# Constants that travel behind the first group's values, and two weight blocks requested by ScalarE

## The chip, the core and the metric

The kernel runs on one NeuronCore of a Trainium2 chip. Its engines work in parallel, each through its own program in order: TensorE (PE, matrix products), VectorE (DVE), ScalarE (ACT), GpSimd (POOL) and SyncE (SP), which here only asks for transfers. The 16 DMA engines move the data. SBUF is the memory on the chip, PSUM the place where TensorE leaves sums. The metric is the device time of one execution in microseconds (us).

## The reference

```python
# retention: q, k, v are (B=4, H=8, S=768, D=64)
gamma = 1.0 - 2.0 ** (-5.0 - np.arange(H))
for t in range(S):
    state = gamma * state + k[t] (outer) v[t]      # per batch and head, D x D
    y[t] = q[t] @ state / sqrt(D)
x = y as (B, S, H * D)                             # 4 x 768 x 512
# gated MLP
h = relu(x @ w_in)                                 # w_in 512 x 1024
u, v = h[..., :512], h[..., 512:]
v_n = (v - mean(v)) / sqrt(var(v) + 1e-6)          # over the last axis
v_s = w_spatial @ v_n + b_spatial                  # w_spatial 768 x 768, over the sequence
out = (u * v_s) @ w_out                            # w_out 512 x 512
```

The weights come to the chip as 64-bit words (doubles) in 12 blocks of 128 x 512 and are split there into a high and a low single-precision part.

## The kernel before

The sequence of each batch is cut into 6 chunks of 128 positions, which makes 24 groups (batch, chunk). For a group two transfers of 512 KB come in: `qk` (keys and queries, transposed) and `vk` (values and keys, natural). The decay of retention is put into scale factors: the values are multiplied by one table before use (`scale_values`), the results by two others at eviction (`out_evict`). These small tables arrive in one transfer, `decay_t` (128 x 80 floats, 40 KB; 320 bytes in each partition). 72 of the 80 columns are the factors for values and for evictions, the last 8 are a compact form of a third table, which is spread on the chip: VectorE multiplies it with an identity pattern (`decay_rows`, output `sown`), TensorE sums it over partitions (`decay_spread`, output `spread`), ScalarE copies the result to `qd_t` (`decay_copy`).

The order of the work is written out by hand in a table, STEPS, of short words. A letter names a step, its digits the group, block or part; every engine runs its own instructions in the order of the words. The words that matter here are: `G` asks for a group's `qk` and `vk`; `v` is the transfer of the constants; `p` scales values (p0 and p1 on GpSimd); `U` gives filling matmuls `wps` on a tile of zeros; `q` and `j` are scores and mask; `L` asks for a block of weights (its tile is `raw`); `a` and `c` are the steps that split it (`room`, `df`), ScalarE first, then VectorE; `m` handles the third table; `t` adds a group to the running sums (`total`), `k` copies these to SBUF (`ws`), `y` makes the outputs (`x`), `E` evicts them (`xf`), `h` and `l` make their high and low parts (`xh`, `xl`), `V` starts the MLP's products.

The words around the change run, before: `G0 v p0 U10 q0 j0 L0 L2 a0 m2 t00 m0 k000 k001 t01 y00`. So ScalarE does a0 (first split step of block 0), then k000 and k001 (copies of the first sums); TensorE does the filling matmuls, q0, t00, m0 (`spread`), t01; and t01, which adds to the same PSUM tile, comes behind the copies of t00. All loads are asked for by SyncE, in the order of the words. Tiles of one tag rotate through a few buffers (`bufs`), so that a load into a buffer waits for the last reader of what was there: `qk` has three, `vk` two. Every third early group takes its `vk` in `third` instead. Large tiles with tags `sp0` to `sp13` hold other things later in the program.

Of the kernel before, what the change touches and what calls it, by code (L numbers as in the profile page):

```python
# [9 lines left out]
F32 = mybir.dt.float32  # L10
# [6 lines left out]
ALU = mybir.AluOpType  # L17
# [4 lines left out]


STEPS = (
# [71 lines left out]
def tile_retention_gmlp(  # L96
# [11 lines left out]
    nc = tc.nc  # L108
    P = 128
    B = out.shape[0]  # L110
    NG = groups.shape[0]
    NC = NG // B
    C = P // 2
    D = C
    NP = groups.shape[3] // (4 * (P // 2))
# [10 lines left out]
    rpool = ctx.enter_context(tc.tile_pool(name="ret", bufs=2))  # L126
# [6 lines left out]
    ND = 3 * NC * NP  # L133
    consts_t = wpool.tile([P, ND + NP * P // C], F32, name="decay_t")
    decay_t = consts_t[:, :ND].rearrange("p (n t h) -> p n t h", t=3, h=NP)
    vd_t, qg_t = decay_t[:, :, :2], decay_t[:, :, 2]
# [2 lines left out]

    mhalf = wpool.tile([P, 1], F32, name="mhalf")  # L140
    nc.gpsimd.memset(mhalf, 0.5)
    nc.scalar.mul(mhalf, mhalf, -1.0)

    winv_w = wpool.tile([P, KT, 2, DM], F32R, name="winv_w")
    winv_h, winv_l = winv_w[:, :, 0], winv_w[:, :, 1]
# [5 lines left out]
    keep = tc.keep_in_program_order  # L151
# [4 lines left out]
    def load(dst, src):  # L156
        keep(nc.sync.dma_start(dst, src))
# [4 lines left out]
    def pick(n):  # L162
        return (nc.gpsimd, nc.vector, nc.scalar)[int(n)]

    doubles = [
        (w[:, k, 0], w[:, k, 1], src[k])
        for w, src in ((winv_w, w_inv), (winu_w, w_inu), (wout_w, w_out))
        for k in range(KT)
    ]
    raws = {}  # L170

    def load_double(i):

        if i >= len(doubles):
            return
        if i < 3:
            if i == 0:
                raws["first"] = mpool.tile([P, 3, DM], I64, tag="vn", name="raw0", bufs=1)
            raws[i] = raws["first"][:, i]
        else:  # L180
            t = slot(STAGED[i], I64, f"raw{i}")
            raws[i] = t.rearrange("p s c -> p (s c)")[:, :DM]
        load(raws[i], doubles[i][2])

    HC = NC // 2

    def slot(n, dtype, name):

        cols = HALF // 2 if dtype == I64 else HALF
        return mpool.tile([P, HC, cols], dtype, tag=f"sp{n}", name=name, bufs=1)  # L190
# [88 lines left out]
    naturals = {}  # L279
    values = {}  # L280
    scores = {}
    states = {}
# [6 lines left out]
    def load_group(g):  # L289
        if g >= NG:  # L290
            return

        t = rpool.tile([P, 2, 2, NP, C], F32, tag="qk", name=f"qk{g}", bufs=3)
        load(t.rearrange("p s i h c -> p (s i h c)"), groups[g, 0])
        keys[g], queries[g] = t[:, 0], t[:, 1]
        if g < EARLY:
            load_values(g)

    EARLY = 9

    def load_values(g):
        if g >= NG:
            return
        if g < EARLY and g % 3 == 2:
            t, w = (
                slot(n, F32, f"third{g}_{n}").rearrange("p s c -> p (s c)")[:, : 4 * NP * C]
                for n in THIRD
            )
            t, w = (x.rearrange("p (s i h c) -> p s i h c", s=2, i=2, h=NP) for x in (t, w))
        else:  # L310
            t = rpool.tile([P, 2, 2, NP, C], F32, tag="vk", name=f"vk{g}", bufs=2)
            w = rpool.tile([P, 2, 2, NP, C], F32, tag="ws", name=f"ws{g}", bufs=2)
        load(t.rearrange("p s i h c -> p (s i h c)"), groups[g, 1])
        values[g], naturals[g] = t[:, 0], t[:, 1]
        scores[g], states[g] = w[:, 0], w[:, 1]

    def scale_values(g, engine=None):
        engine = engine or nc.gpsimd
        if engine is nc.scalar:
            for i in range(2):  # L320
                for hp in range(NP):
                    v, f = values[g][:, i, hp], vd_t[:, g % NC, i, hp : hp + 1]
                    keep(nc.scalar.mul(v, v, f))  # L323
            return
        vd = vd_t[:, g % NC].unsqueeze(3).broadcast_to([P, 2, NP, D])
        keep(engine.tensor_tensor(values[g], values[g], vd, ALU.mult))  # L326

    total = {}
# [384 lines left out]
    def warm(n):  # L713
# [3 lines left out]
    splits = split_clamp, split_shift, split_sign, split_power, split_low  # L717

    steps = {
        "m": lambda n: (decay_spread, decay_copy, decay_rows)[n](),  # L720
        "v": lambda n: load(consts_t, decay),
        "B": lambda n: load(bsp_t, b_sp),
        "L": load_double,
        "K": load_spatial,
        "G": load_group,
        "J": load_values,
        "a": split_top,
        "c": lambda n: splits[n % 10](n // 10),
        "H": split_high,
        "R": lambda n: split_rest(n % 100, pick(n // 100)),  # L730
        "Q": lambda n: split_sum(n % 100, pick(n // 100)),
        "p": lambda n: scale_values(n % 100, pick(n // 100)),
        "q": ret_scores,
        "j": ret_mask,
# [59 lines left out]
            eye_t[r], eye_t[r], [[1, C]], ALU.is_equal, 0.0, base=0, channel_multiplier=-1  # L794
        )

    def decay_rows():
        n = NP * P // C
        eye = eye_t.unsqueeze(2).broadcast_to([P, C, n])
        own = consts_t[:, ND:].unsqueeze(1).broadcast_to([P, C, n])  # L800
        rows = rows_t.rearrange("p (c n) -> p c n", n=n)
        keep(nc.vector.tensor_tensor(rows, eye, own, ALU.mult))

    def decay_spread():
        spread[0] = ps_m.tile([P, NP * P], F32, tag="m", name="spread")
# [6 lines left out]
    for n in ROOMS:  # L812
        t = slot(n, F32, f"room{n}").rearrange("p s c -> p (s c)")
        rooms += [t[:, :DM], t[:, DM : 2 * DM]]

    for word in STEPS.split():
        steps[word[0]](int(word[1:] or 0))

# [85 lines left out]
```

## Time and profile before

| What | Value |
|---|---|
| median of 3 runs | 371.31 us (370.73 to 371.78) |
| the profiled execution | 370.93 us |
| its span, first to last instruction | 369.1 us |
| busy: TensorE, VectorE, ScalarE, GpSimd | 362.0, 240.1, 155.8, 114.2 us |
| granted TensorE clock, mean | 0.999 |
| moved by DMA | 41.20 MB, 112 GB/s over the span |

The busy times say that TensorE has almost no room. They are sums over the whole program; whether the start has other limits than the rest is seen only in views of single stretches.

### The profile page before, as it was taken

The page shows a single profiled execution, that of the slowest core. Times are in us where ns is not written, and L with a number is a line of the kernel's source. Part 1 is how long each engine was busy: PE and PEld are TensorE (multiplying, and loading weights), DVE is VectorE, ACT ScalarE, POOL GpSimd, SP SyncE. Part 2 cuts the span into 40 slices and gives each one's busy share as a digit, 9 for nine tenths or more (in the row PEclk, how much of TensorE's full clock was granted, in tenths as well). Part 3 has the DMA queues.
Part 4 walks back from the last instruction along what each step waited for, and adds up shares of the span by engine and source line. Part 5 has one row for each costly group of instructions (what it writes and reads, how often), then busy time and mean ns, then how long its engine had stood idle before and what let it go on. Part 6 is the DMA issues. An engine that isn't in the chain of part 4 may idle for free.

```text
span 369.1 us, 10329 instructions
## 1 busy us (share of the span) xinstructions
PE 362.0 (98%) x4428; PEld 315.1 (85%) x4428; DVE 240.1 (65%) x533; ACT 155.8 (42%) x321; POOL 114.2 (31%) x121
## 2 busy tenths in 40 slices
PE   7999999999999999999999999999999999999995
PEld 3678885879888889999988889999998888999884
DVE  2998999599866767797685563278585443165631
ACT  2798784443512455532223246242133244433232
POOL 3612621461053325243225341233142321404010
PEclk9999999999999999999999999999999999999999
DMA  7975886012343430303333114113304002000022
GB/s 279 409 263 202 290 333 247 0 33 83 103 158 115 173 123 24 116 2 115 115 117 143 58 59 144 44 73 115 118 0 141 6 0 87 0 0 2 1 87 85
DMA packets 13149, 41.20 MB, mean 112 GB/s; under 512 B 1584, under 2 KB 1840, under 8 KB 13104
## 3 DMA queue, kind: packets, MB, share of 16 engines
q1 hardware_dynamic: 12960, 40.42, 30.4%
q8 instruction: 35, 0.57, 0.7%
q10 hardware_dynamic: 144, 0.13, 0.1%
q14 instruction: 10, 0.08, 0.1%
HBM read 34.25 MB, written 6.29 MB: 110 GB/s over the span
## 4 chain that ended last, share of the span: by engine, by line
PE 96%; ACT 1%; DVE 1%; issue 0%; DVEq 0%
PE u L154 18%; PE v L154 18%; PE o L154 18%; PE y L154 10%; PE sp L154 8%; PE x L154 6%; PE z L154 5%; PE s L154 4%; PE w L154 3%; PE d L154 3%; PE wps L715 2%; PE total L154 1%; ACT third L323 1%; PE o_last L154 0%; ACT third L352 0%
## 5 line engine op out<-in xcount | busy, mean ns | idle before, releaser
L154 PE MATMUL u<-xh,winu_w 128*128 128x384 f32 x256 | 68.3, 338 | 0.0
L154 PE MATMUL v<-winv_w,xh 128*128 128x512 f32 x192 | 60.8, 398 | 0.0
L154 PE MATMUL o<-wout_w,gh 128*128 128x512 f32 (+1 forms) x192 | 59.7, 392 | 0.0
L449 DVE SCALAR_TENSOR_TENSOR xf<-x,decay_t,qd_t 128x128 f32<-128x128 f32 x96 | 29.2, 344 | 28.7 <-PE x L154 23.9
L154 PEld LDWEIGHTS u<-xh,winu_w 128*128 128x128 f32 x256 | 46.5, 188 | 0.7
L154 PE MATMUL u<-xl,winu_w 128*128 128x384 f32 x128 | 42.9, 335 | 0.0
L154 PE MATMUL y<-sp,a 128*128 128x384 f32 x216 | 42.1, 338 | 0.0
L154 PEld LDWEIGHTS v<-winv_w,xh 128*128 128x128 f32 x192 | 35.2, 188 | 7.5
L154 PEld LDWEIGHTS o<-wout_w,gh 128*128 128x128 f32 x192 | 35.2, 188 | 6.9
L547 POOL TENSOR_TENSOR vn<-vn 128x384 f32<-128x384 f32 x24 | 24.9, 1036 | 50.5 <-DVE a L160 41.6
L563 ACT CAST a<-vn 128x384 fp32r<-128x384 f32 x42 | 21.0, 512 | 42.8 <-POOL vn L547 27.3
L154 PEld LDWEIGHTS y<-sp,a 128*128 128x128 f32 x216 | 37.9, 188 | 0.5
L154 PE MATMUL v<-winv_w,xl 128*128 128x512 f32 x96 | 37.6, 392 | 0.0
L154 PE MATMUL o<-wout_w,gl 128*128 128x512 f32 (+1 forms) x96 | 37.3, 389 | 0.0
L326 POOL TENSOR_TENSOR vk<-vk,decay_t 128x512 f32<-128x512 f32 x18 | 19.7, 1094 | 39.4 <-DMA vk<-in_float_dram 35.8
L160 DVE TENSOR_TENSOR a<-vn,a 128x384 fp32r<-128x384 f32 x42 | 23.8, 580 | 12.5 <-ACT a L563 12.3
L513 POOL TENSOR_TENSOR rs<-rs,mhalf 128x1 f32<-128x1 f32 x24 | 15.0, 629 | 50.2 <-DVE rs L509 47.8
L624 ACT ACTIVATE ur<-u 128x384 f32<-128x384 f32 x32 | 15.2, 488 | 36.0 <-PE u L154 32.4
L500 DVE BATCH_NORM_STATS2 bst<-vr 128x6 f32<-128x512 f32 x24 | 16.4, 686 | 18.4 <-ACT vr L493 18.4
L154 PE MATMUL s<-qk 64*64 64x64 f32 x768 | 28.2, 221 | 0.0
L154 PEld LDWEIGHTS s<-qk 64*64 64x64 f32 x768 | 25.4, 136 | 2.7 <-issue 2.3
L402 DVE TENSOR_TENSOR ws<-d,ws 64x256 f32<-64x256 f32 x54 | 22.8, 422 | 6.5 <-PE d L154 5.0
(114 smaller groups left out, 671.7 us busy)
## 6 DMA issues: line engine op xcount, KB each, us to landing
qk<-in_float_dram SPq DMA_DIRECT2D x24, 512.0 KB, 4.8
vk<-in_float_dram SPq DMA_DIRECT2D x21, 512.0 KB, 4.6
raw<-in_int_dram SPq DMA_DIRECT2D x12, 512.0 KB, 6.9
out_dram<-ot SPq DMA_DIRECT2D x23, 256.0 KB, 2.1
wst<-in_float_dram SPq DMA_DIRECT2D x4, 576.0 KB, 8.6
third<-in_float_dram SPq DMA_DIRECT2D x3, 512.0 KB, 10.0
bsp_t<-in_float_dram SPq DMA_DIRECT2D x1, 384.0 KB, 6.8
out_dram<-ot SPq DMA_DIRECT2D x1, 128.0 KB, 2.0
```

Source lines behind the costliest of these rows:

```text
L154: keep(nc.tensor.matmul(out, lhs, rhs, start=start, stop=stop, skip_group_check=shared))
L160: return eng.tensor_tensor(out, whole, high.bitcast(F32), ALU.subtract)
L323: keep(nc.scalar.mul(v, v, f))
L326: keep(engine.tensor_tensor(values[g], values[g], vd, ALU.mult))
L402: keep(nc.vector.tensor_tensor(dst[ROWS[r]], u, states[g][ROWS[r], i], ALU.add))
L449: nc.vector.scalar_tensor_tensor(xf[:, hp], t[hp % 2][:, hp // 2].rearrange("p i c -> p (i c)"), qg_t[:, c, hp : hp + 1], qd_t[:, hp], ALU ...
L500: keep(nc.vector.bn_stats(st, norm[b, c][0]))
L513: keep(nc.gpsimd.tensor_tensor(rs, rs, mhalf, ALU.pow))
L547: nc.gpsimd.tensor_tensor(*{7: (a11, a11, a21, ALU.subtract), 5: (a21, a21, a22, ALU.add), 6: (a21, a22, a11, ALU.subtract), 3: (a21, a12, ...
L563: keep(nc.scalar.copy(t[:, 0], part_whole(b, p, m)))
L624: keep(nc.scalar.activation(u, pu[:, :HALF], AF.Relu))
L715: keep(nc.tensor.matmul(wps, wz[:, :P], wz, start=True, stop=True))
```

## The change

The constants lose their own transfer. The host puts them behind group 0's values, so that one transfer brings 1104 floats in each partition instead of 1024. Its tile, `values0`, is no `vk` buffer but a room with tag `sp8`. GpSimd's p0 and VectorE's `decay_rows` read the constants there; for all later readers ScalarE copies 80 columns to `decay_t` (word `v`, now `consts_copy`). Weight blocks 0 and 2 are asked for by ScalarE, ahead of all its other work, with its table load and the product on `mhalf` behind; their words L0 and L2 leave the table. The word m2 becomes m102, which names VectorE as its engine, as before. (Two pieces of the table, then the code.)

```diff
-    "G0 v p0 U10 q0 j0 L0 L2 a0 m2 t00 m0 k000 k001 t01 y00 U301 y01 c00 c01 c02 c03 a2 c20 c21 "
+    "G0 v p0 U10 q0 j0 a0 m102 t00 m0 k000 k001 t01 y00 U301 y01 c00 c01 c02 c03 a2 c20 c21 c22 "
...
     mhalf = wpool.tile([P, 1], F32, name="mhalf")
     nc.gpsimd.memset(mhalf, 0.5)
-    nc.scalar.mul(mhalf, mhalf, -1.0)
...
-        load(raws[i], doubles[i][2])
+        if i in (0, 2):
+            keep(nc.scalar.dma_start(raws[i], doubles[i][2]))
+        else:
+            load(raws[i], doubles[i][2])
...
     EARLY = 9
+    ROOM0 = 8
+
+    first = {}
+
+    def consts_copy():
+        keep(nc.scalar.copy(consts_t, first[0][:, 4 * NP * C :]))
 
     def load_values(g):
         if g >= NG:
+            return
+        if g == 0:
+            t = slot(ROOM0, F32, "values0").rearrange("p s c -> p (s c)")
+            t = first[0] = t[:, : 4 * NP * C + ND + NP * P // C]
+            load(t, decay)
+            t = t[:, : 4 * NP * C].rearrange("p (s i h c) -> p s i h c", s=2, i=2, h=NP)
+            w = rpool.tile([P, 2, 2, NP, C], F32, tag="ws", name=f"ws{g}", bufs=2)
+            values[g], naturals[g] = t[:, 0], t[:, 1]
+            scores[g], states[g] = w[:, 0], w[:, 1]
             return
...
-        vd = vd_t[:, g % NC].unsqueeze(3).broadcast_to([P, 2, NP, D])
+        vd = vd_t[:, g % NC]
+        if g == 0:
+            vd = first[0][:, 4 * NP * C : 4 * NP * C + ND]
+            vd = vd.rearrange("p (n t h) -> p n t h", t=3, h=NP)[:, 0, :2]
+        vd = vd.unsqueeze(3).broadcast_to([P, 2, NP, D])
...
-        "v": lambda n: load(consts_t, decay),
+        "v": lambda n: consts_copy(),
...
-        own = consts_t[:, ND:].unsqueeze(1).broadcast_to([P, C, n])
+        own = first[0][:, 4 * NP * C + ND :].unsqueeze(1).broadcast_to([P, C, n])
...
+    load_double(0)
+    load_double(2)
+    keep(nc.scalar.mul(mhalf, mhalf, -1.0))
     for word in STEPS.split():
...
+    head = arrays["groups"][0, 1], arrays["decay"], qd.reshape(P, -1).astype(np.float32)
+    arrays["decay"] = np.concatenate(head, 1)
```

SyncE's first requests, before (`raw` are weight blocks, `qk` and `vk` the groups in turn, `third` is group 2's):

```order
L157 DMA qk_98<-in_float_dram 128x1024
L157 DMA vk_100<-in_float_dram 128x1024
L157 DMA decay_t<-in_float_dram 128x80
L157 DMA raw_133<-in_int_dram 128x512 x2
L157 DMA qk_196<-in_float_dram 128x1024
L157 DMA vk_198<-in_float_dram 128x1024
L157 DMA raw_133<-in_int_dram 128x512
L157 DMA qk_252<-in_float_dram 128x1024
```

SyncE's first requests with the change:

```order
L156 DMA qk_101<-in_float_dram 128x1024
L156 DMA values_103<-in_float_dram 128x1104
L156 DMA qk_196<-in_float_dram 128x1024
L156 DMA vk_198<-in_float_dram 128x1024
L156 DMA raw_97<-in_int_dram 128x512
L156 DMA qk_252<-in_float_dram 128x1024
```

The constants and two weight blocks have left this queue; group 1's two transfers stand directly behind group 0's.

ScalarE's first instructions, before (`room` is the first split step of a block, `ws` the copies of sums):

```order
L142 ACT_TABLE_LOAD
L142 ACTIVATE mhalf<-mhalf 128x1
L200 ACTIVATE room_96<-raw_133 128x512
L352 COPY ws_101<-total 64x256 x2
L200 ACTIVATE room_97<-raw_133 128x512
L352 COPY ws_199<-total 64x256 x2
L234 CAST winv_w<-df_188 128x512
L809 COPY qd_t<-spread 128x512
```

ScalarE's first instructions with the change:

```order
L183 DMA raw_97<-in_int_dram 128x512 x2
L841 ACT_TABLE_LOAD
L841 ACTIVATE mhalf<-mhalf 128x1
L307 COPY decay_t<-values_103 128x80
L202 ACTIVATE room_95<-raw_97 128x512
L373 COPY ws_105<-total 64x256 x2
L202 ACTIVATE room_96<-raw_97 128x512
L373 COPY ws_199<-total 64x256 x2
```

Two requests now stand ahead of everything, and the copy of the constants stands ahead of the first split step. The instructions of TensorE, VectorE and GpSimd keep their order; some read another tile.

## Rows read from the trace of the kernel before

**Rows 1.** The profile's page, part 4: the chain that ended last, by engine.

```profile
PE 96%; ACT 1%; DVE 1%; issue 0%; DVEq 0%
```

**Rows 2.** Waits of TensorE over the span: us in total, times, longest.

```profile
...
PE total L154 <- ACT ws L352: 0.9, 1, 0.9
...
```

**Rows 3.** Windows: busy us of each engine, granted clock, DMA share, GB/s.

```profile
core 0: us, PE busy (x) PEld busy (x) DVE busy (x) ACT busy (x) POOL busy (x), PEclk, DMA share, GB/s
5.60:22.00 16.40, 14.37 (x372) 10.77 (x375) 14.04 (x29) 11.73 (x30) 6.76 (x5) 1.00 0.98 380
1.75:4.75 3.00, 3.00 (x9) 1.08 (x8) 0.00 (x0) 0.53 (x2) 0.72 (x4) 1.00 0.96 326
4.75:6.00 1.25, 1.25 (x9) 0.41 (x9) 0.00 (x0) 0.00 (x0) 0.00 (x0) 1.00 0.92 257
6.00:10.00 4.00, 3.21 (x66) 2.18 (x68) 2.51 (x5) 1.92 (x4) 1.04 (x1) 1.00 1.00 393
```

**Rows 4.** Timeline of SyncE from the start: start us, us, request.

```profile
0.80 0.37 SPq L157 DMA_DIRECT2D qk<-in_float_dram  x1
1.23 0.41 SPq L157 DMA_DIRECT2D vk<-in_float_dram  x1
1.69 0.42 SPq L157 DMA_DIRECT2D decay_t<-in_float_dram  x1
2.16 0.91 SPq L157 DMA_DIRECT2D raw<-in_int_dram  x2
```

**Rows 5.** DMA issues, single requests in order: KB, us from issue to landing.

```profile
qk<-in_float_dram SPq DMA_DIRECT2D x1, 512.0 KB, 3.8
vk<-in_float_dram SPq DMA_DIRECT2D x1, 512.0 KB, 4.6
raw<-in_int_dram SPq DMA_DIRECT2D x1, 512.0 KB, 6.6
```

**Rows 6.** Timeline of all engines, 0 to 16 us (idle before, and its releaser).

```profile
0.79 1.28 ACT L142 ACT_TABLE_LOAD   x1 [0.79 <-PEq L876]
...
1.25 4.45 PE L715 MATMUL wps<-wz 128*128 128x512 bf16 x10 [1.25 <-DVE wz L775]
...
5.62 1.42 PE L154 MATMUL s<-qk 64*64 64x64 f32 x32
...
6.22 1.04 POOL L326 TENSOR_TENSOR vk<-vk,decay_t 128x512 f32<-128x512 f32 x1 [3.60 <-DMA decay_t<-in_float_dram]
...
7.32 0.68 PE L154 MATMUL total<-vk 64*64 64x64 f32 x16 [0.28 <-POOL vk L326]
7.78 0.68 DVE L802 TENSOR_TENSOR sown<-sown,decay_t 128x512 f32<-128x512 f32 x1
8.02 0.66 ACT L200 ACTIVATE room<-raw 128x512 f32<-128x512 f32 x1 [5.73 <-DMA raw<-in_int_dram]
...
8.52 1.12 PE L154 MATMUL spread<-sown 128*128 128x512 f32 x2 [0.52 <-DVE sown L802]
8.70 0.74 ACT L352 COPY ws<-total 64x256 f32<-64x256 f32 x2
...
11.37 0.82 PE L715 MATMUL wps<-wz 128*128 128x512 bf16 x3
...
11.91 1.30 POOL L326 TENSOR_TENSOR vk<-vk,decay_t 128x512 f32<-128x512 f32 x1 [4.65 <-DMA vk<-in_float_dram]
```

**Rows 7.** The chain that ended last, in order of time: start us, us.

```profile
9.64 0.44 PE total L154 x10
...
13.26 0.71 PE total L154 x15
```

**Rows 8.** DMA view of 4.75 to 6.00 us: packets by size.

```profile
DMA packets 206, 0.32 MB, mean 257 GB/s; under 512 B 136, under 2 KB 136, under 8 KB 206
```

**Rows 9.** Timeline of ScalarE, 11 to 22 us: group 2's scaling.

```profile
16.70 2.02 ACT L323 ACTIVATE third<-third,decay_t 128x64 f32<-128x64 f32 x8
```

**Rows 10.** DMA issues, 364 us to the end: the last two stores of 128 KB.

```profile
out_dram<-ot SPq DMA_DIRECT2D x1, 128.0 KB, 2.0
out_dram<-ot_last ACTq DMA_DIRECT2D x1, 128.0 KB, 2.3
```

More of the change, by code (lines that the diff above doesn't have):

```diff
@@ L719, in tile_retention_gmlp @@
     steps = {
-        "m": lambda n: (decay_spread, decay_copy, decay_rows)[n](),
-        "v": lambda n: load(consts_t, decay),
+        "m": lambda n: (
+            decay_rows(pick(n // 100)) if n % 100 == 2 else (decay_spread, decay_copy)[n]()
+        ),
+        "v": lambda n: consts_copy(),
         "B": lambda n: load(bsp_t, b_sp),
@@ L795, in tile_retention_gmlp, with decay_rows @@
         )
-    def decay_rows():
+    def decay_rows(engine):
         n = NP * P // C
         eye = eye_t.unsqueeze(2).broadcast_to([P, C, n])
-        own = consts_t[:, ND:].unsqueeze(1).broadcast_to([P, C, n])
+        own = first[0][:, 4 * NP * C + ND :].unsqueeze(1).broadcast_to([P, C, n])
         rows = rows_t.rearrange("p (c n) -> p c n", n=n)
-        keep(nc.vector.tensor_tensor(rows, eye, own, ALU.mult))
+        keep(engine.tensor_tensor(rows, eye, own, ALU.mult))
     def decay_spread():
@@ L871 @@
         "b_sp": np.broadcast_to(moe_b_spatial.reshape(1, S), (P, S)),
-        "decay": np.concatenate(
-            [np.concatenate([vdecay, qg], 2).reshape(P, -1), qd.reshape(P, -1)], 1
-        ).astype(np.float32),
-    }
+        "decay": np.concatenate([vdecay, qg], 2).reshape(P, -1).astype(np.float32),
+    }
+    head = arrays["groups"][0, 1], arrays["decay"], qd.reshape(P, -1).astype(np.float32)
+    arrays["decay"] = np.concatenate(head, 1)
     nc = _bacc.Bacc("TRN2", target_bir_lowering=False, num_devices=1, dynamic_dma_scratch_size=1024)
```

50 rows, old and new, of the table STEPS are left out of this document.

## The prediction

> **What bounds the kernel now.** I read the page first: the chain of work that ended last lies on TensorE for 96% [rows 1]. That is a mean over two stages, so the view of TensorE's waits comes next. Over the whole span it has five groups, none later than 22 us; the longest single wait but the first start is 0.9 us [rows 2]. From 5.6 to 22 us, in contrast, TensorE is busy 14.37 of 16.40 us while the DMA engines are busy 0.98 of the time [rows 3]. So the end comes as much later or earlier as TensorE's work reaches about 22 us later or earlier. What is cheaper on another engine after that is worth nothing, and a delay before it counts one for one.
>
> The first 22 us are a chain, which the timelines give. SyncE asks for transfers one behind another [rows 4]. Request plus time to landing is [rows 4, 5]: first qk 0.80 + 3.8 = 4.6 us, vk 1.23 + 4.6 = 5.8, second raw 2.6 + 6.6 = 9.2; it is asked for in the second half of the pair that starts at 2.16. decay_t is seen in who waits for it: GpSimd scales group 0's values from 6.22 on, released by decay_t, for 1.04 us; in the same way ScalarE's first split step at 8.02 shows the first raw, and GpSimd's second scaling at 11.91 group 1's vk [rows 6]. TensorE's sums of group 0 (`total`, step t00) start at 7.32 and take 0.68. Then comes the matmul `spread` at 8.52, after 0.52 us of idling for VectorE's `sown` [rows 6], and behind it t01, at 9.64 in the chain. From there TensorE goes through fixed work (products, four filling matmuls, group 1's scores) to group 1's sums at 13.26 [rows 7].
>
> **The change, part by part.**
>
> *SyncE asks for less.* The requests for decay_t (0.42 us) and two of the raws (0.91) leave SyncE's queue [rows 4], so everything behind is asked for some 1.3 us sooner. That alone brings nothing: from 1.75 us on the DMA engines are busy 0.92 to 1.00 of the time [rows 3], and an earlier request waits in a full queue. What does bring time is the loss of the 40 KB transfer. From 4.75 to 6.00 us the rate falls to 257 GB/s, where it is 393 in the stretch behind [rows 3], and 136 of that stretch's 206 packets are under 512 bytes [rows 8]; decay_t has 128 rows of 320 bytes. Its price is 1.25 x (1 - 257/393) = 0.43 us. The constants' 320 bytes now lengthen rows of 4 KB: the same bytes without the small packets. What lands later therefore lands about 0.4 us sooner.
>
> *ScalarE asks for two blocks.* Two requests, about 0.42 us each as on SyncE, stand ahead of its table load (1.28) and the product on mhalf. All this ends near 3 us, and ScalarE idles until 8.02 [rows 6], so it is hidden. mhalf is read only in the later normalization.
>
> *The landing of the values, V.* This decides. Before, 512 KB of queries and keys and then 512 KB of values had the DMA engines to themselves. Now 1 MB of raws is asked for beside them, from 0.79 us on, when ScalarE starts [rows 6], with SyncE at 0.80 [rows 4]. No row shows two loading queues side by side. Bound from below: the values follow the first 512 KB with nothing between, V = 5.8, as vk did. Bound from above: all four transfers are through before the values are complete; that was 9.2 for the second raw, less 0.43, V = 8.8. Between them: the engines are full, so a second asker adds no bandwidth but takes some. Both lists hold about 1 MB and neither asks first, so with equal shares in small pieces they end together, near the upper bound. If the low rate of the start, 326 against 393 GB/s [rows 3], came from having one asker, they end up to 3.00 x (1 - 326/393) = 0.5 us sooner, at 8.3. I take V = 8.45, within 8.3 to 8.8.
>
> The Trainium skill, "DMA: Bandwidth & Descriptors", section "Issuing engines are not separate DMA queues", speaks against what the edit seems to aim at: requests from several engines run on the same 16 DMA engines and interleave, and only issuing time is saved. Its section "Queues, rings and completion order" has each DMA engine go round the queues packet by packet. By that rule the sum is the one with the late V; if ScalarE's requests were served behind SyncE's, it would be nearly no change. No row of this case shows it.
>
> *What a late V costs.* GpSimd starts at V + 0.06 and takes 1.04; t00 starts at V + 1.17 and takes 0.7; `sown` (0.68 on VectorE) now needs only the same landing and is ready by V + 0.75, so its 0.52 us of waiting is gone; `spread` takes 1.12 [rows 6]; t01 starts at about V + 2.98. Before, it was 9.64 [rows 7]. So the loss is **V - 6.66**, nothing up to V = 6.7, and with V = 8.45 it is **1.8 us**. ScalarE must keep up: it now copies the constants behind V, at most about 0.3 us by the products of 128x64 (2.02/8 = 0.25, [rows 9]), then does the first split step (0.66), all over by V + 1.0. The copies of the sums that t01 waits for start at V + 1.9 and take 0.74 [rows 6], until V + 2.65, ahead of V + 2.98: hidden, with 0.3 to spare. VectorE's split of the first raw starts about 0.8 later than now; it stands ahead of the first eviction, which waits for ScalarE's copy of `spread` and comes later by the whole loss anyway.
>
> *Does anything behind absorb it?* Group 1's sums at 13.26 stand behind group 1's scores, but also need GpSimd's scaling, over at 11.91 + 1.30 = 13.21 [rows 6, 7]. That one comes 0.4 us sooner while TensorE is late, so perhaps 0.1 us comes back. ScalarE's scaling of group 2 at 16.70 has no idle time ahead of it [rows 9]: it waits for ScalarE's own queue and not for DMA, and moves with the rest. After that the chain alternates among ScalarE, VectorE and TensorE, all late alike, until 22 us. No buffer helps: group 0 no longer takes a `vk` buffer, so group 3's load loses one wait, but it stands in SyncE's queue behind group 3's qk, which waits for group 0's last products, now later.
>
> *Sum:* +1.8 - 0.1 = **+1.7 us**. The profiled execution took 370.93, which gives 372.6. The median of the runs is 371.31, 0.38 above it, so I forecast **373.0**. Its own range, from V = 8.3 to 8.8, is +1.5 to +2.1, or 372.8 to 373.4. A measurement here can tell about 0.3% (1.1 us) from no change, which is V near 7.9.
>
> **The rivals.**
>
> *Turns by whole transfers, SyncE's first.* Each DMA engine does its share of qk, then raw, then values, then raw. The values are third, where the first raw was: 8.0 - 0.43 = 7.5. Loss 0.9, time 372.2: within the bound. For it: in one queue transfers land whole, 1.2 us apart for the first two [rows 4, 5]. Against it: if ScalarE's come first on any engine, V is 8.8 again, since a landing waits for the slowest of 16.
>
> *Not slower: SyncE's transfers get through first.* One mechanism: ScalarE's queue starts late or gets a smaller share, and the values land by V = 6.7. The loss is then nothing, and up to 0.3 us comes back because group 1's values land sooner: 371.0 to 371.3. It decides below V = 6.7. For it: the requests come from different engines, and one may take longer to start. Against it: ScalarE's only request of before landed 2.3 us after its issue, beside 2.0 for SyncE's of the same size [rows 10], so its queue isn't slow. Even V = 5.8 wins little, since t01 hangs on the scores, the mask and `sown` (from 5.62 until `spread` at 8.52, [rows 6]), none of which starts sooner.
>
> *TensorE's clock falls.* The first ten filling matmuls took 4.45 us, three later ones 0.82 [rows 6], 0.445 against 0.27 each: the pace of the lower level (1.2 GHz), then of the upper (2.4 GHz), though the granted clock is recorded as 1.00 [rows 3]. With V = 8.45 TensorE idles from about 7.2 to 9.6 us, where it had two waits of 0.3 and 0.5 [rows 6]. If the clock falls there, the 3.6 us from t01 to group 1's sums (9.64 to 13.26, [rows 7]) take up to twice as long: between 0 and 3.6 us more. I put it at 1.5, time 374.5. Against it: with waits of up to 0.9 us the whole of 5.6 to 22 us is granted 1.00 [rows 2, 3].
>
> *A gain that I don't see:* transfers that land 0.4 us sooner in many places. After 22 us nothing on TensorE's chain waits for one.
>
> **How the numbers follow.** Equal shares, +1.7: 0.52. Whole turns, +0.9: 0.18. SyncE first, 0 to -0.3: 0.14. Clock fall on top: 0.10. A gain: 0.06. Slower by over 0.3%: the first and the fourth and a little of the second, 0.64. Within: most of the second and the third, 0.30. Faster: 0.06. The range reaches from "SyncE first" to "clock falls": 371.2 to 374.5; it leaves out about 0.1 below and 0.07 above.
>
> **What would show it.** GpSimd's first scaling starts when the values land: near 8.5 if right, near 6 if SyncE came first, 7.6 with whole turns. The first qk lands about 1.2 us later than its 4.6 with equal shares. t00 and `spread` stand back to back without the 0.52 us wait; t01 starts near 11.4, group 1's sums near 15.0. The packets under 512 bytes are gone from the first 6 us. From 24 us on TensorE waits for nothing. I am wrong if V is under 7.8, or if TensorE still idles after 24 us, so that a delay is absorbed.

## The result and the profile after

The change makes the kernel slower: 374.23 us (373.57 to 375.15, 6 runs) against 371.53 (370.73 to 371.86, 6 runs), a ratio of 1.0074 with a 95% interval of 1.0045 to 1.0102, or 2.7 us. I had forecast 373.0, within 371.2 to 374.5, and slower at 0.64. The profiled execution took 374.06 us.

The page of the changed kernel, its first line and the chain by engine:

```profile
span 372.1 us, 10325 instructions
...
PE 94%; DMA 2%; ACT 1%; DVE 1%; POOL 0%; issue 0%; SPq 0%; POOLq 0%
```

The chain has a new member. In [rows 1] DMA did not appear; now 2% of the span is one transfer, `values`. The DMA issues of the first 2 us, single requests (KB, us from issue to landing):

```profile
raw<-in_int_dram ACTq DMA_DIRECT2D x1, 512.0 KB, 4.6
qk<-in_float_dram SPq DMA_DIRECT2D x1, 512.0 KB, 4.4
...
values<-in_float_dram SPq DMA_DIRECT2D x1, 552.0 KB, 6.7
...
raw<-in_int_dram ACTq DMA_DIRECT2D x1, 512.0 KB, 7.2
```

SyncE's qk and ScalarE's raw, both asked for at 0.80, land at 5.2 and 5.4; SyncE's values and ScalarE's second raw, asked for at about 1.23, at 7.9 and 8.4. The two queues advance side by side at about equal speed. The values needed V = 1.23 + 6.7 = 7.93 us, where vk and the constants were there by 6.2 before [rows 4 to 6]. The raws gained what the values lost: the first came at 8.0 before [rows 6], and it now lies there from 5.4 on and waits for ScalarE.

The rate in the windows of [rows 3]:

```profile
1.75:4.75 3.00, 3.00 (x9) 1.07 (x8) 0.00 (x0) 1.45 (x2) 0.71 (x4) 1.00 0.94 349
4.75:6.00 1.25, 1.25 (x10) 0.41 (x9) 0.00 (x0) 0.00 (x0) 0.00 (x0) 1.00 1.01 396
```

The dip to 257 GB/s from 4.75 to 6.00 us is gone, as forecast, and the start is somewhat quicker, 349 instead of 326. Now the engines, which answer to [rows 6] (timeline of the changed kernel, 0 to 18 us):

```profile
0.80 0.89 ACTq L183 DMA_DIRECT2D raw<-in_int_dram  x2
...
5.62 1.57 PE L153 MATMUL s<-qk 64*64 64x64 f32 x32
...
8.07 0.69 DVE L825 TENSOR_TENSOR sown<-sown,values 128x512 f32<-128x512 f32 x1
8.12 1.54 POOL L347 TENSOR_TENSOR values<-values 128x512 f32<-128x512 f32 x1 [5.49 <-DMA values<-in_float_dram]
8.16 0.66 ACT L202 ACTIVATE room<-raw 128x512 f32<-128x512 f32 x1
8.85 1.09 DVE L207 TENSOR_SCALAR room<-room 128x512 f32<-128x512 f32 x1
...
9.71 0.92 PE L153 MATMUL total<-values 64*64 64x64 f32 x16 [2.52 <-POOL values L347]
...
10.56 2.07 PE L153 MATMUL spread<-sown 128*128 128x512 f32 x2
```

Three things are to be seen. GpSimd's scaling starts at 8.12, and it takes 1.54 us where it took 1.04. TensorE idles 2.52 us for it. And then `spread` takes 2.07 us where it took 1.12. The reason for the last is in the granted clock (windows of TensorE alone: us, busy, PEclk, DMA share, GB/s):

```profile
8.00:10.00 2.00, 0.29 (x9) 1.00 1.01 414
10.00:13.00 3.00, 3.00 (x24) 0.50 1.03 416
13.00:14.00 1.00, 0.85 (x30) 0.79 1.01 401
```

For 3 us and more the clock stands at 0.50, the lower of its two levels, 1.2 GHz, right behind the idle stretch. In the chain, in order of time (start us, us):

```profile
9.71 0.92 PE total L153 x16
10.63 2.00 PE spread L153 x2
12.63 0.73 PE total L153 x10
...
24.61 1.16 PE x L153 x64
```

t01 starts at 12.63 where it started at 9.64 [rows 7], 3.0 us later. Group 2's products `x` start at 24.61, 3.0 later than in the chain of the kernel before:

```profile
21.64 1.16 PE x L154 x64
```

The span ends 3.0 later, 372.1 for 369.1. Nothing on the way absorbs anything. The 3.0 split into 1.27 for the landing (7.93 - 6.66), 0.13 for GpSimd's start (0.19 behind the landing instead of 0.06), 0.5 for its longer scaling, and 1.1 for `total` and `spread` at the lower clock (0.92 + 2.00 - 0.70 - 1.12).

### The profile page after: what moved, and what is told of

It is laid out like the page before. It is cut to its first block, busy times and chain, and to the rows that moved or that the text cites. A ratio compares the mean times of both kernels' runs of the same rounds, so it can differ in the third digit from the quotient of the medians.

```text
span 372.1 us, 10325 instructions
## 1 busy us (share of the span) xinstructions
PE 362.9 (98%) x4425; PEld 315.7 (85%) x4428; DVE 240.5 (65%) x533; ACT 155.8 (42%) x322; POOL 114.8 (31%) x121
## 3 DMA queue, kind: packets, MB, share of 16 engines
q10 hardware_dynamic: 432, 1.18, 0.8%
## 4 chain that ended last, share of the span: by engine, by line
PE 94%; DMA 2%; ACT 1%; DVE 1%; POOL 0%; issue 0%; SPq 0%; POOLq 0%
PE u L153 18%; PE v L153 18%; PE o L153 18%; PE y L153 10%; PE sp L153 8%; PE x L153 6%; PE z L153 5%; PE s L153 3%; PE w L153 3%; PE d L153 3%; DMA values<-in_float_dram 2%; PE total L153 1%; PE spread L153 1%; ACT third L340 1%; POOL values L347 0%; PE o_last L153 0%
## 5 line engine op out<-in xcount | busy, mean ns | idle before, releaser
L159 DVE TENSOR_TENSOR a<-vn,a 128x384 fp32r<-128x384 f32 x42 | 23.6, 575 | 12.8 <-ACT a L584 12.6
```

Of the source, the lines that this page charges most:

```text
L159: return eng.tensor_tensor(out, whole, high.bitcast(F32), ALU.subtract)
```

## The experiments

The lines of the table are shown up to m102 or m2; what follows in them is unchanged.

**One half each.** The merge alone (all requests by SyncE again):

```diff
-    "G0 v p0 U10 q0 j0 a0 m102 ...
+    "G0 v p0 U10 q0 j0 L0 L2 a0 m102 ...
...
-        if i in (0, 2):
-            keep(nc.scalar.dma_start(raws[i], doubles[i][2]))
-        else:
-            load(raws[i], doubles[i][2])
+        load(raws[i], doubles[i][2])
...
-    load_double(0)
-    load_double(2)
```

> The constants travel behind the values, but SyncE asks for all weight blocks in their old places. Theory (the whole loss comes from ScalarE's two requests, which take bandwidth from the values): the values land near 6.0 us, GpSimd starts its scaling there, t01 stays near 9.6 us, and the time is that of the kernel before, 371.2 to 371.6. Rival (the merge itself costs, through p0 and decay_rows reading one tile at the same time, or through ScalarE's copy): t01 at 10 us or later and 372 or more.

Measured: 371.17 us, ratio 0.9984 (0.9962 to 1.0007): no loss. Timeline of that run:

```profile
4.83 1.15 PE L153 MATMUL s<-qk 64*64 64x64 f32 x32
...
5.62 1.04 POOL L344 TENSOR_TENSOR values<-values 128x512 f32<-128x512 f32 x1 [2.99 <-DMA values<-in_float_dram]
...
7.45 1.12 PE L153 MATMUL spread<-sown 128*128 128x512 f32 x2
```

The values are there before 5.6 us, 0.6 sooner than the constants were. t01 was expected near 9.6 and came at 8.6, because in this execution the ten filling matmuls ended early: the scores start at 4.83 instead of 5.62. Such shifts of the start come and go from run to run (the ten runs go from 369.86 to 372.12), so the median is what counts here.

The other half, the kernel before with ScalarE's two requests only:

```diff
-    "G0 v p0 U10 q0 j0 L0 L2 a0 m2 ...
+    "G0 v p0 U10 q0 j0 a0 m2 ...
...
-    nc.scalar.mul(mhalf, mhalf, -1.0)
...
-        load(raws[i], doubles[i][2])
+        if i in (0, 2):
+            keep(nc.scalar.dma_start(raws[i], doubles[i][2]))
+        else:
+            load(raws[i], doubles[i][2])
...
+    load_double(0)
+    load_double(2)
+    keep(nc.scalar.mul(mhalf, mhalf, -1.0))
     for word in STEPS.split():
```

> The kernel before, with its own transfer for the constants, but ScalarE asks for weight blocks 0 and 2 ahead of all else. Theory (sharing of bandwidth): values and constants land at 7.9 to 8.4 us, t01 at 12.6 or a little later, 374.2 to 374.6. Rival (the merge is needed for the loss): under 372.5.

Measured: 374.16 us, ratio 1.0083 (1.0054 to 1.0111). Here the scaling waits for the transfer of the constants:

```profile
8.42 1.52 POOL L328 TENSOR_TENSOR vk<-vk,decay_t 128x512 f32<-128x512 f32 x1 [5.79 <-DMA decay_t<-in_float_dram]
```

So the whole loss comes from the requests, and the merge neither makes nor mends it. The time is as forecast, 0.04 under its range, the way there only in part: t01 stands at 11.78 in the chain and not at 12.6, because the clock fell only at 11.5, 1.5 us after TensorE had resumed, when `spread` had run at the upper level (1.18 us). Group 2's `x` stands at 24.74 all the same, 3.1 later than before.

**One request instead of two.** The changed kernel, with block 2 back on SyncE:

```diff
-    "G0 v p0 U10 q0 j0 a0 m102 ...
+    "G0 v p0 U10 q0 j0 L2 a0 m102 ...
...
-        if i in (0, 2):
+        if i == 0:
...
     load_double(0)
-    load_double(2)
```

> The changed kernel, but ScalarE asks for weight block 0 alone; SyncE asks for block 2 in its old turn, behind the values. Theory (two queues share the DMA engines in equal small pieces): qk and raw land together near 5.3 us as in the changed kernel, then the values have the engines to themselves and land near 6.7; by the line V - 6.66 nothing is lost, t01 at 9.6 to 10.0, time 371.2 to 372.0. Rival (any request by ScalarE ahead of the values costs what two cost): values at 7.9, 374.

Measured: 371.68 us, ratio 1.0002 (0.9991 to 1.0014), as the theory had it. DMA issues of that kernel, single requests:

```profile
values<-in_float_dram SPq DMA_DIRECT2D x1, 552.0 KB, 5.6
```

Its timeline:

```profile
6.96 1.04 POOL L347 TENSOR_TENSOR values<-values 128x512 f32<-128x512 f32 x1 [4.33 <-DMA values<-in_float_dram]
...
8.67 1.13 PE L153 MATMUL spread<-sown 128*128 128x512 f32 x2
```

The values land at 1.23 + 5.6 = 6.8, 6.7 was forecast, and t01 starts at 9.72. The 0.5 MB taken off ScalarE brought the values forward by 1.1 us. The profiled run ends 0.7 later than the one of before all the same, at 369.8; 0.5 of that is a new wait of TensorE for GpSimd's `xl`.

**The clock.** TensorE's idle stretch is filled with matmuls on zeros, ten of them (the first line with a plus), then six (the second):

```diff
-    "G0 v p0 U10 q0 j0 a0 m102 ...
+    "G0 v p0 U10 q0 U210 j0 a0 m102 ...
+    "G0 v p0 U10 q0 U106 j0 a0 m102 ...
```

> The changed kernel, with ten more filling matmuls behind group 0's scores, where TensorE idled from 7.2 to 9.7 us. At the upper level they take 2.2 us, so they end before the scaled values are there. Theory (about 1.1 to 1.3 of the 3.0 us are the lower clock between 10 and 13.3 us): granted clock 1.00 throughout, spread takes 1.1 instead of 2.0, t01 near 11.4, time 372.8 to 373.2. Rival (the clock is not what costs, the chain through ScalarE and VectorE is late anyway): 373.9 or more with the clock at 1.00.

> The kernel with ten fillers in the gap, with six instead, so that they end before the scaled values are there. Theory (clock): granted clock 1.00 up to 22 us, t01 at 11.1 to 11.4, and if the stall of 1.7 us near 31 us (in which TensorE waits for nothing that the profile shows) goes with the smaller program, 372.2 to 372.8. Rival: the stall stays and with it 373.3.

Measured: 373.34 us, ratio 1.0053 (1.0034 to 1.0073) with ten, 374.42 us, ratio 1.0082 (1.0060 to 1.0103) with six. In both the granted clock was 1.00 throughout and `spread` took 1.12 us; t01 started at 11.34 and 11.60 instead of 12.56, and group 2's `x` at 23.13 and 23.30 instead of 24.61. With ten, t00 started no sooner than in the changed kernel (9.67 for 9.71), since the fillers ended only then; so what t01 gained is the clock. At `x` the gain is 1.3 to 1.5 us, but the median is only 0.9 lower with ten and 0.2 higher with six, outside what was expected of either. Timeline of the kernel with ten:

```profile
10.28 1.12 PE L153 MATMUL spread<-sown 128*128 128x512 f32 x2
...
11.34 0.51 PE L153 MATMUL total<-values 64*64 64x64 f32 x10
...
31.93 0.50 PE L153 MATMUL v<-winv_w,xh 128*128 128x512 f32 x1 [1.68 <-issue]
```

At 31.93 TensorE had stood for 1.7 us and waited for nothing that the profile shows; with six it is 1.4 us, at 32.9. The theory held up to 24 us and failed for the time.

The same ten matmuls as in the changed kernel, only divided otherwise, keep the program's length:

```diff
-    "G0 v p0 U10 q0 j0 a0 m102 ...
+    "G0 v p0 U4 q0 U106 j0 a0 m102 ...
```

> The changed kernel with its ten filling matmuls divided: four ahead of group 0's scores, six behind them, so that TensorE's program is no longer than before. Theory (the stall of 1.3 to 1.7 us near 32 us in the three kernels with added fillers comes with the longer program, and the lower clock costs about 1.3): no such stall, granted clock 1.00 from 9 us on, t01 at 11.2 to 11.6, time 372.6 to 373.1. Rival (the stall follows from the later or earlier start of the work and not from its length): the stall stays, 373.9 to 374.5.

Measured: 372.93 us, ratio 1.0038 (1.0020 to 1.0056), by the medians 1.3 us below the changed kernel (whose interval, 1.0045 to 1.0102, overlaps), without that stall. Timeline:

```profile
7.21 2.74 PE L736 MATMUL wps<-wz 128*128 128x512 bf16 x6
...
8.19 1.54 POOL L347 TENSOR_TENSOR values<-values 128x512 f32<-128x512 f32 x1 [5.57 <-DMA values<-in_float_dram]
...
9.88 0.98 PE L153 MATMUL total<-values 64*64 64x64 f32 x16
10.79 1.13 PE L153 MATMUL spread<-sown 128*128 128x512 f32 x2
```

And the clock in the windows in which the changed kernel had 0.50 and 0.79:

```profile
10.00:13.00 3.00, 2.76 (x50) 1.00 1.03 412
13.00:14.00 1.00, 0.99 (x34) 1.00 1.04 414
```

With the landing as late (8.1) and GpSimd as slow (1.54), `spread` is back at 1.13 us, t01 starts at 11.84 and group 2's `x` 1.1 sooner, at 23.53. So the clock is worth about 1.1 to 1.3 us here. t01 was expected at 11.2 to 11.6; it is later because the six fillers ran slowly too (2.74) and ended behind the scaling. At 0.46 us each, with `total` at 0.98, they have the pace of the lower level, though the granted clock is recorded as 1.00. By its pace TensorE came to the upper level only between `total` and `spread`, so this run shows no clock that held through the wait.

**GpSimd's scaling.** VectorE does it instead, alone (the first line with a plus) and then with six fillers (the second):

```diff
-    "G0 v p0 U10 q0 j0 a0 m102 ...
+    "G0 v U10 q0 j0 p100 a0 m102 ...
+    "G0 v U10 q0 U106 j0 p100 a0 m102 ...
```

> The changed kernel, with VectorE instead of GpSimd scaling group 0's values, behind its mask. GpSimd took 1.54 us for it where it took 1.04 before; VectorE needs about 0.69. Theory (0.5 of the loss is GpSimd slowed by VectorE beside it): t00 at 8.8 us instead of 9.71, spread at 9.5; TensorE idles 1.6 us only; time 372.2 to 372.6 if the clock then holds, 373.2 if it falls all the same. Rival (the scaling is no part of the path): no change, 374.2.

> VectorE scales the values of group 0, and six filling matmuls stand behind group 0's scores. Theory (the three parts add up: late values, slow scaling on GpSimd, lower clock): spread takes 1.1 us instead of 2.07, t01 near 10.7 instead of 11.84, time 371.2 to 372.0, what is left being the late values alone. Rival (clock and scaling overlap, so that only one counts): 372.4 as with VectorE alone.

Measured: 372.44 us, ratio 1.0026 (1.0014 to 1.0038) alone; 373.22 us, ratio 1.0045 (1.0030 to 1.0059) with fillers. Timeline with VectorE alone:

```profile
8.04 0.69 DVE L347 TENSOR_TENSOR values<-values 128x512 f32<-128x512 f32 x1 [0.68 <-DMA values<-in_float_dram]
...
8.79 1.12 PE L153 MATMUL total<-values 64*64 64x64 f32 x16 [2.25 <-DVE values L347]
...
9.83 2.07 PE L153 MATMUL spread<-sown 128*128 128x512 f32 x2
```

The scaling is on the path: t00 starts 0.9 us sooner, and the time falls by 1.8 us at an unchanged landing. In the profiled run the clock fell here too, behind 2.2 us of idling (1.6 were expected), and its time, 372.37, is well under the 373.2 forecast for that case. The mean granted clock of the runs says more: it is 0.991 to 0.995 in all six of the changed kernel, but 0.995 in only four of these ten (median 372.64) and 0.998 to 1.000 in the other six (372.25). So part of the 1.8 is a clock that mostly held, and in this kernel the clock is worth about 0.4 us of the whole time. Only the profiled run shows where it fell, and why it is worth so little here is open. With fillers it did not fall, and t01 started at 10.53, close to the forecast 10.7, so up to there the parts add up. But of the 1.3 us gained at t01 only 0.3 were left at group 2's `x` (23.24 against 23.54); 0.6 of the difference is a wait of TensorE for GpSimd's `xl`. And the stall came again:

```profile
32.55 0.50 PE L153 MATMUL v<-winv_w,xl 128*128 128x512 f32 x1 [1.26 <-issue]
```

The time of the second kernel is a miss.

**A version below both.** Merge without ScalarE's requests, and eight filling matmuls ahead of the scores (U8 for U10); beside it the kernel before with eight. The first pair of lines is on the merge alone, the second on the kernel before:

```diff
-    "G0 v p0 U10 q0 j0 L0 L2 a0 m102 ...
+    "G0 v p0 U8 q0 j0 L0 L2 a0 m102 ...
...
-    "G0 v p0 U10 q0 j0 L0 L2 a0 m2 ...
+    "G0 v p0 U8 q0 j0 L0 L2 a0 m2 ...
```

> Constants behind the values, all requests by SyncE, and eight filling matmuls instead of ten ahead of group 0's scores. In the run with the merge alone TensorE's clock happened to rise early, the scores started at 4.83 us instead of 5.62, and the whole came 0.8 us sooner. Theory (with the merge the scores are what the start hangs on, no longer the constants): scores at 4.7 to 4.9, spread near 7.5, time 370.2 to 370.9, below both kernels. Rival (with fewer fillers the clock rises later and takes the gain back): 371.2 or more.

> The kernel before, with eight filling matmuls instead of ten ahead of group 0's scores. Theory (the constants still land at 6.1, so the scaling starts at 6.2 and t00 at 7.3; only the wait for sown goes): spread at 8.0, 370.8 to 371.3, half of the gain that the merge with eight fillers has. Rival (the fillers alone are the gain): 370.3, like the merge with eight.

Measured: 370.30 us, ratio 0.9965 (0.9952 to 0.9977) with the merge, and 371.20 us, ratio 1.0002 (0.9970 to 1.0034), without. Timeline with the merge:

```profile
4.51 1.15 PE L153 MATMUL s<-qk 64*64 64x64 f32 x32
...
5.69 1.04 POOL L344 TENSOR_TENSOR values<-values 128x512 f32<-128x512 f32 x1 [3.06 <-DMA values<-in_float_dram]
...
7.40 1.12 PE L153 MATMUL spread<-sown 128*128 128x512 f32 x2
```

In these profiled runs the merge is worth something once SyncE keeps its order. The scores start sooner with fewer fillers in both kernels (4.51 and 4.76); what the merge adds is that the transfers behind the constants land sooner. ScalarE splits the first block from 6.84 instead of 7.90, so its copies, and with them t01, come sooner (8.45 for 9.39), and group 1's values are scaled from 10.86 instead of 11.79. Without it, fewer fillers give 0.1 us at group 1's sums (13.16 for 13.26; 12.10 with the merge). With it the start hangs on the values again and not on the scores: TensorE waits 1.1 us for their scaling. The two intervals just overlap, so the gain over fewer fillers alone is not quite clear of noise. The profiled run of the kernel without the merge had a stall too:

```profile
32.70 0.27 PE L154 MATMUL s<-qk 64*64 64x64 f32 x1 [1.14 <-issue]
```

Its program is shorter than that of before, so a longer program is not what brings the stall.

## Why the prediction was right, and where its sizes were off

*What bounds the kernel* held. In the changed kernel a delay of 3.0 us at t01 is one of 3.0 at 24 us and of 3.0 at the end.

*SyncE asks for less* held: the dip went, and raws and group 1's values came sooner, to no use on the path while group 0's were late.

*ScalarE asks for two blocks*: the requests are hidden on ScalarE itself, as forecast: they take 0.89 us, and it idles until 8.0.

*The landing V* was right in kind: equal shares, shown by the landings of qk and raw and by the experiment with one block, which moved V to where this said. In size I took 8.45, within 8.3 to 8.8, and it was 7.93, below that range. I had taken the middle of two assumptions on the rate; the start was faster than before (349 for 326 GB/s), all four transfers were through by 8.4, and the values ended 0.5 us ahead of the second raw. The first qk landed at 5.2, 0.6 later than its 4.6 and not 1.2. The line V - 6.66 gives 1.27 with that instead of 1.8. Whole turns and "SyncE first" are out: qk and the first raw landed 0.2 us apart, and the values neither at 7.5 nor at 6.

*What a late V costs* has the step that failed: "GpSimd starts at V + 0.06 and takes 1.04". It started at V + 0.19 and took 1.54. I had seen that `sown` now needs only the same landing, and credited the wait that goes away, but not that both engines then start on one tile at once. Where VectorE was first, by 0.05 us in the changed kernel and in the one with moved fillers, `sown` took 0.69 and GpSimd 1.54. In the kernel with ten fillers GpSimd was first (timeline of that run):

```profile
8.10 1.04 POOL L347 TENSOR_TENSOR values<-values 128x512 f32<-128x512 f32 x1 [5.47 <-DMA values<-in_float_dram]
...
8.21 1.48 DVE L825 TENSOR_TENSOR sown<-sown,values 128x512 f32<-128x512 f32 x1
```

In each of these runs the second of the two waits for the first: 1.54 - 1.04 = 0.5 lost when GpSimd comes second, 1.48 - 0.69 = 0.8 when VectorE does. The Trainium skill, "SBUF — State Buffer", section "Who interferes with whom", says that a VectorE instruction with two inputs in SBUF contends with a GpSimd instruction that reads SBUF, for ports that only one of them holds at a time, and that issue order decides which of the two blocks. The traces agree, but for 0.14 us: waiting until the other is over would have cost 8.76 - 8.12 = 0.64 and 9.14 - 8.21 = 0.93.

*The clock* was a rival at 0.10, priced at 1.5 on top. It came true, at 1.1 to 1.3 up to group 2's `x`. My argument against it, that waits of up to 0.9 us had left the clock alone [rows 2], did not reach to a wait of 2.5 us, so putting the clock at nothing in the sum was the second step that failed.

So the forecast of +1.7 was 1.8 for V less 0.1, and the profile has 1.27 + 0.13 + 0.5 + 1.1 for +3.0 in the profiled runs, and +2.7 in the medians. The 0.1 that group 1's earlier values were to give back did not come. The error in V and what I had left out pulled in opposite ways, which is luck. The range held because it reached to the clock.

The stall of 1.1 to 1.7 us near 32 us stood in the profiled runs of three kernels with added fillers and one with fewer, and in none of the others. The traces say where: each time TensorE stood right after its 603rd weight load, whatever the work there, and went on 2.4 to 2.5 us after a packet of the instruction queue q8. In the kernel with ten fillers that packet is at 29.55 (DMA view of 29.50 to 29.75, then the timeline of the weight loads):

```profile
q8 instruction: 1, 0.02, 26.1%
...
31.93 0.19 PEld L153 LDWEIGHTS v<-winv_w,xh 128*128 128x128 f32 x1 [2.12 <-issue]
```

In the eight kernels without the stall the 604th weight load also comes 2.3 to 3.2 us after such a packet, but there TensorE reached its 603rd 1.7 us or more behind the packet; with the stall it did so 0.1 to 1.1 behind, and the sooner, the longer it stood. So TensorE most likely waits for its next instructions, and part of what a faster start gains is lost there. Open: no run moved the packet by itself, and why it comes when it does is not shown.

## What to carry to other kernels

A request moved to an idle engine's queue cost nothing to issue here (0.89 us in which ScalarE had nothing to do), but it is a claim on the same full DMA engines: what the first steps wait for must have the first bytes to itself, and what is needed later must be asked for later. When two operations are given one common start (here both released by one landing), look whether VectorE and GpSimd then collide. And price a longer wait of TensorE with its clock: in the changed kernel, behind 2.5 us of waiting, it cost about 1.2 us more up to 24 us. In the whole time it was worth about 0.4 us (VectorE's scaling) to 1.3 us (moved fillers), and nothing where TensorE then waited for instructions or another engine instead (six fillers).

## What the runs showed of the hardware

Two loading queues share the DMA engines about evenly: 512 KB each, asked for in the same 0.1 us, landed at 5.2 and 5.4 us, and one alone in front at 4.6 in the kernel before (0.80 + 3.8, [rows 5]) and at 4.1 (0.80 + 3.3) in the run with the merge alone, DMA issues:

```profile
qk<-in_float_dram SPq DMA_DIRECT2D x1, 512.0 KB, 3.3
```

The granted clock fell to 0.50 behind idle stretches of TensorE of 2.2, 2.5 and 3.6 us (the last with ScalarE's requests only); it stayed at 1.00 behind one of 2.1 us that had six fillers ahead of it (the kernel with six), and behind all shorter ones. It is also recorded as 1.00 in the first microseconds of every trace, where the pace of the fillers is that of the lower level, so behind the 2.2 us in which the kernel with moved fillers waited for qk it says nothing.
